# Decay factors made on the chip from three bfloat16 parts, weight slots placed by name, start and end reordered

## The chip, the cores and the metric

The kernel runs on one core of a Trainium2 chip. The metric is the device time of one execution in microseconds (us). Engines are called TensorE (PE in the rows, its weight loads PEld), VectorE (DVE), ScalarE (ACT), GpSimd (POOL) and SyncE (SP, which issues most of the DMAs). L12 is line 12 of the kernel before.

## What is computed

Three layers in a row, all in float32 at the border: retention (attention with a decay in place of the softmax), a mixture of eight experts with a skip, and a gated linear layer (GLU) with weights in float64. Cut to what matters:

```python
# retention: q, k, v are (4, 8, 576, 64)
scores = q @ k.transpose(0, 1, 3, 2) / sqrt(64)
gamma = 1 - 2.0 ** (-5.0 - arange(8))
ret = scores * where(i >= j, gamma ** (i - j), 0)
x = (ret @ v), as 2304 rows of 512
# experts: w1 (8, 512, 1024), w2 (8, 1024, 512)
for rows with x @ w_skip > 0:
    e = argmax(x @ w_gate); g = softmax(x @ w_gate)[e]
    x = x + g * (relu(x @ w1[e]) @ w2[e])
# GLU: w_a, w_b (512, 1536), w_out (1536, 512)
out = ((x @ w_a) * (x @ w_b)) @ w_out
```

## The kernel before

**Retention.** 18 tiles of 128 rows, nine to a pair of batches. The decay gamma^(i-j) is split: k is scaled by gamma^(-s) ahead of the transposes (`scale_k`, line 629, on GpSimd), and the output of a tile is multiplied by gamma^s / 8 (`decay`, line 721, VectorE). These second factors, `qt_sb`, are a table of 128 partitions by 4 head pairs by 576 positions in float32, 1.18 MB. It is loaded in four pieces (lines 758, 770, 773, 776). Tile i runs `scores` (line 673, then the mask product of line 676), q's transposes of a later pair of tiles (line 639, evicted in lines 647 on VectorE and 649 on ScalarE), k's transposes of tile i+1 (line 661, ScalarE eviction), `emit_x` of tile i-1 (line 741), `values` (lines 711 and 716) and `state` (line 691). A load of q serves two tiles.

**Start.** Lines 752 to 790 are written out by hand. All loads go through SP's queue, in this order: the key scales of consts_a, k of tile 0, consts (with the identity), q of tiles 0 and 1, the masks of consts_a, v, a table piece, k of tile 1, the routing weights, and so on. VectorE sets tiles to zero, ScalarE copies the identity into `xl_rhs`. TensorE multiplies an idle tile (`keep_warm`, line 134) eight times, transposes k, multiplies once more, transposes q in two halves, multiplies twice more, and then enters the loop.

**Experts.** Each expert runs the order of a plan, a string of names that `run_expert` goes through: F0 to F7 are the first products (line 503), S0 to S7 and Q0 to Q7 the second products for the first 128 rows and the 64 others (lines 517 and 535), E0 and E1 their evictions, X0 and X1 the transposes of the next expert's rows, N a gather, f, t and s the fetch, transposes and split of the GLU's first rows. `l` loads a quarter of a weight matrix of a later expert (line 202, 512 KB), `L` loads a piece of a GLU weight into a staging place (line 222, 512 KB), `gs` starts turning a staged piece into two fp32r parts and `gp` goes one step on with it. 36 such pieces make nine units of four. `split_wide` (lines 235 to 257) takes a piece of float64 apart with six VectorE instructions and three of ScalarE.

**Weight places.** Eight places of 8 KB a partition (`slots_a`) are taken in turn: expert e uses four, expert e+2 the same four again, so `l` in expert e loads for expert e+2. GLU units 0 to 4 have places of their own, units 5 to 8 take the turns after the last expert's, two each: units 5 and 6 the places of expert 6, units 7 and 8 those of expert 7. Up to 26 pieces may start before the GLU (`early`, line 1122).

**GLU.** Six groups of three tiles, twelve steps each. `glu_in` makes both products of a step (line 1239), ScalarE copies one (line 1243), VectorE multiplies (line 1244), and `split2` makes two fp32r parts (line 464 on ScalarE, line 465 on VectorE, in the first four steps on GpSimd). Then up to two remaining pieces are started and finished on the spot (`piece_pair(2)`, line 1291), and after that come the output products of the step before (`glu_out`, line 1256). The last step evicts three tiles (lines 1261 and 1263) and stores them from SP's queue; the last of them, tile 17, needs two transfers.

## Time and profile before

| | us |
|---|---|
| median of 3 runs | 766.37 |
| lowest, highest | 765.18, 767.53 |
| the profiled execution | 766.19 |
| its span, first to last instruction | 764.4 |
| TensorE busy in it | 745.5 |
| VectorE, ScalarE, GpSimd busy | 305.6, 230.1, 103.4 |
| DMA | 93.81 MB |

The busy time of TensorE is modelled at the ends of matmuls, so a full TensorE is not TensorE at its peak. In a row of a timeline the first number is the start in us from the span's start, the second the length of the merged group, and a bracket gives the idle time ahead of it and what ended that time. The granted clock is a share of 2.4 GHz.

### The profile page before, as it was taken

What the parts mean: (1) busy time and instruction counts of PE and PEld (TensorE: products, weight loads), DVE (VectorE), ACT (ScalarE), POOL (GpSimd) and SP (SyncE); (2) the same over time, 40 slices, a digit from 0 to 9 for tenths busy, and PEclk for the clock granted to TensorE, in tenths of its full rate; (3) what the DMA queues carried; (4) which work ended last, traced back from release to release, by engine and by line L of the source; (5) the groups of instructions that cost most, each with busy time, mean ns of one, the idle gap of its engine ahead of it and who ended that gap; (6) DMA issues with size and microseconds to landing.
All of it is one profiled execution on the core that took longest, in us unless ns stands there. A gap on an engine that the chain in (4) does not pass through costs nothing.

```text
span 764.4 us, 11767 instructions
## 1 busy us (share of the span) xinstructions
PE 745.5 (98%) x4753; PEld 652.8 (85%) x4753; DVE 305.6 (40%) x658; ACT 230.1 (30%) x482; POOL 103.4 (14%) x132
## 2 busy tenths in 40 slices
PE   8999998999999999999999999999999999999997
PEld 5889886766677777979999999999999999999996
DVE  5557664665666174982222222222222222222111
ACT  3445431444444153651221222121212121212111
POOL 1221111232211110140040004000400030001000
PEclk9999999999999999999999999999999999999999
DMA  9979997599998722440040004000400020001001
GB/s 229 228 189 251 276 318 260 182 380 360 343 347 302 223 78 75 136 140 1 1 124 0 1 1 125 1 0 1 124 4 25 14 83 1 1 1 42 1 1 41
DMA packets 89370, 93.81 MB, mean 123 GB/s; under 512 B 44833, under 2 KB 66977, under 8 KB 89314
## 3 DMA queue, kind: packets, MB, share of 16 engines
q1 hardware_dynamic: 84210, 78.07, 32.2%
q0 software_dynamic: 5104, 14.98, 6.3%
q8 instruction: 38, 0.62, 0.3%
q14 instruction: 18, 0.15, 0.1%
HBM read 80.02 MB, written 13.01 MB: 122 GB/s over the span
## 4 chain that ended last, share of the span: by engine, by line
PE 76%; DVE 3%; DMA 2%; issue 0%; ACT 0%; SPq 0%; ACTq 0%; DVEq 0%
PE ab L1239 36%; PE o L1256 18%; PE h L503 10%; PE y L517 6%; PE yr L535 4%; DMA st<-in_moe_w_out_dram 1%; PE pt L1104 1%; DVE mh L248 1%; PE xt L479 1%; DVE w L251 1%; DVE mh L243 1%; PE h L559 0%; DVE hb L241 0%; DMA y_dram<-yo 0%; DVE hb L252 0%
## 5 line engine op out<-in xcount | busy, mean ns | idle before, releaser
L1239 PE MATMUL ab<-xt,w 128*128 128x384 f32 x1728 | 313.0, 335 | 0.0
L1239 PEld LDWEIGHTS ab<-xt,w 128*128 128x128 f32 x1728 | 303.2, 188 | 6.5 <-issue 0.4
L1256 PE MATMUL o<-w,gg 128*128 128x512 f32 x648 | 163.5, 396 | 1.9 <-ACT gg L464 1.4
L1244 DVE TENSOR_TENSOR a_sb<-ab,a_sb 128x384 f32<-128x384 f32 x72 | 40.1, 557 | 276.0 <-PE ab L1239 250.9
L1256 PEld LDWEIGHTS o<-w,gg 128*128 128x128 f32 x648 | 119.2, 188 | 25.7 <-ACT gg L464 2.1
L1243 ACT ACTIVATE a_sb<-ab 128x384 f32<-128x384 f32 x72 | 35.3, 490 | 178.3 <-PE ab L1239 171.1
L464 ACT ACTIVATE gg<-a_sb 128x384 fp32r<-128x384 f32 x72 | 37.9, 526 | 163.6 <-DVE a_sb L1244 163.6
L503 PE MATMUL h<-xe,w 128*128 128x192 f32 x448 | 75.1, 328 | 0.0
L503 PEld LDWEIGHTS h<-xe,w 128*128 128x128 f32 x448 | 72.5, 190 | 3.0 <-issue 2.7
L517 PE MATMUL y<-w,ht 128*128 128x512 f32 x128 | 59.4, 598 | 0.0
L444 POOL DMA_INDIRECT out_dram<-ob,turns x15 | 14.8, 989 | 313.7 <-ACT ob L1263 311.5
L465 DVE TENSOR_TENSOR gg<-a_sb,gg 128x384 fp32r<-128x384 f32 x68 | 38.0, 559 | 40.3 <-ACT gg L464 37.9
L517 PEld LDWEIGHTS y<-w,ht 128*128 128x128 f32 x128 | 22.8, 190 | 20.3 <-issue 19.9
L251 DVE TENSOR_TENSOR w<-hb,st 128x512 fp32r<-128x512 f32 x36 | 24.8, 690 | 33.7 <-ACT st L246 33.4
L245 ACT ACTIVATE hb<-hb,ebias 128x512 int32<-128x512 int32 x36 | 25.8, 717 | 30.5 <-DVE hb L241 27.2
L438 POOL DMA_INDIRECT xg<-x_dram,list_i x15 | 15.0, 998 | 106.8 <-PE xt L479 56.7
L629 POOL TENSOR_TENSOR ks<-k,cst_a 128x512 f32<-128x512 f32 x18 | 18.8, 1043 | 78.0 <-DMA k<-in_k_dram 42.5
L506 ACT ACTIVATE ht<-h 128x384 f32<-128x384 f32 (+1 forms) x32 | 15.2, 475 | 45.1 <-PE h L503 45.1
L676 DVE TENSOR_TENSOR At<-s,cst_a 128x512 f32<-128x512 f32 x36 | 23.1, 684 | 10.6 <-PE s L673 10.6
L257 DVE TENSOR_TENSOR w<-mh,hb 128x512 fp32r<-128x512 f32 x36 | 24.3, 688 | 5.6 <-ACT mh L250 4.5
L535 PEld LDWEIGHTS yr<-w,ht 128*64 128x64 f32 x224 | 15.5, 137 | 12.4 <-DVE mh L248 3.8
L535 PE MATMUL yr<-w,ht 128*64 128x256 f32 x224 | 25.7, 382 | 0.0
(153 smaller groups left out, 639.8 us busy)
## 6 DMA issues: line engine op xcount, KB each, us to landing
w<-in_moe_w_dram SPq DMA_DIRECT2D x64, 512.0 KB
st<-in_moe_w_a_dram SPq DMA_DIRECT2D x12, 512.0 KB
st<-in_moe_w_b_dram SPq DMA_DIRECT2D x12, 512.0 KB
st<-in_moe_w_out_dram SPq DMA_DIRECT2D x12, 512.0 KB
x_dram<-xs SPq DMA_DIRECT2D x18, 256.0 KB
k<-in_k_dram SPq DMA_DIRECT2D x16, 256.0 KB
q<-in_q_dram SPq DMA_DIRECT2D x8, 512.0 KB
v<-in_v_dram SPq DMA_DIRECT2D x16, 256.0 KB
```

The costliest lines, as they stand in the source:

```text
L245: nc.scalar.activation(out=hb, in_=hb, func=ACTF.Relu, scale=8.0, bias=ebias)
L251: nc.vector.tensor_tensor(out=hi, in0=hb.bitcast(F32), in1=wh.bitcast(F32), op=ALU.mult)
L257: nc.vector.tensor_tensor(out=lo, in0=ml, in1=hb.bitcast(F32), op=ALU.mult)
L464: nc.scalar.activation(out=dst_hi, in_=src, func=ACTF.Copy)
L465: lo_engine.tensor_tensor(out=dst_lo, in0=src, in1=dst_hi, op=ALU.subtract)
L503: nc.tensor.matmul(ph[b][:, i], lhsT=w[:, c0:c0 + P], rhs=xh[:, kd], start=(kd == 0), stop=(kd == KD - 1), skip_group_check=True)
L517: nc.tensor.matmul(py[0], lhsT=ht[f][:, :P], rhs=w[:, f % 4], start=(f == 0), stop=(f == 7))
L535: nc.tensor.matmul(py[0][j * REST:(j + 1) * REST], lhsT=ht[f][:, at:at + REST], rhs=w[:, f % 4, j * half:(j + 1) * half], start=(f == 0), ...
L1239: nc.tensor.matmul(p, lhsT=w[a][:, kd, fc:fc + P], rhs=xt2[g][b][kd // 2][:, kd % 2], start=(j == 0), stop=(j == 3 * KD - 1))
L1243: nc.scalar.activation(out=a_sb, in_=pab[0], func=ACTF.Copy)
L1244: nc.vector.tensor_tensor(out=a_sb, in0=pab[1], in1=a_sb, op=ALU.mult)
L1256: nc.tensor.matmul(po[g][t], lhsT=gg[:, a, t * P:(t + 1) * P], rhs=w[b][:, f % 4], start=(f == 0 and j == 0), stop=(f == NF - 1 and j == 2))
```

## The change

**Decay factors.** The table is no longer loaded. Each factor is written on the host as three bfloat16 parts that sum to it exactly; a 24-row table of parts (8 heads by 3) with a 24-row selector of ones is loaded, 60 KB. Before the attention TensorE multiplies selector and table, 512 and 64 columns for each of four head pairs, and VectorE and ScalarE copy the sums from PSUM into `qt_sb`.

**Start.** k of tile 0 and q come first on SP's queue, q in two halves. The key scales, the part table, the identity and the masks come on ScalarE's queue; the rest of consts goes to SP behind the loads of tile 3. The memsets, the identity copies and `ut_bf` move to GpSimd, the first key scaling to VectorE. The idle products become 5, 2, 2 and 2. For tile 0 each half of q's transposes is evicted by both engines.

**Places by name.** Each weight unit has a fixed place. Expert 7 takes expert 6's four places, not expert 5's, so that GLU units 5 and 6 take those of expert 5, units 7 and 8 those of expert 7. Expert 5's plan loses its `l`. Up to 30 pieces may start before the GLU, and the plans of the last experts start and load them at other points. A strip of 120 floats (`rim`), which nothing used, goes.

**Pieces.** The scaling on ScalarE goes into VectorE's product. In the GLU one piece a step is started instead of two, and all subtractions of line 465 run on VectorE.

**End.** The last step takes its tiles in the order 2, 0, 1; the last one is evicted in halves by VectorE and ScalarE and stored from two queues.

```diff
+T_SEL = 0
+T_TAB = NP * P
+T_N = 5 * 256
...
-    slots_a = ctx.enter_context(tc.tile_pool(name="slots_a", bufs=NA))
+    slots_a = ctx.enter_context(tc.tile_pool(name="slots_a", bufs=1))
...
+    holder = [None] * NA
+    place = {n: (n % NA if n < 4 * (E - 1) else (n - 4) % NA) for n in range(4 * E)}
+    places_g = {}
+    for j, n in enumerate((4 * (E - 3), 4 * (E - 3) + 2, 4 * (E - 1), 4 * (E - 1) + 2)):
+        places_g[NB + j] = place[n], place[n + 1]
...
-    def turn_free(turn):
-        return turn == turns_taken[0] and (turn < NA or turn - NA in used)
...
+    def slot_free(n):
+        return holder[n] is None or holder[n] in used
+
+    def take_slot(n, dtype, who):
+        holder[n] = who
+        return slots_a.tile([P, 4, 512], dtype, tag=f"w{n}", name="w")
...
-        nc.scalar.activation(out=ml, in_=ml, func=ACTF.Copy, scale=2.0 ** -20)
...
-        nc.vector.tensor_tensor(out=lo, in0=ml, in1=hb.bitcast(F32), op=ALU.mult)
+        nc.vector.scalar_tensor_tensor(out=lo, in0=ml, scalar=2.0 ** -20, in1=hb.bitcast(F32),
+                                       op0=ALU.mult, op1=ALU.mult)
...
+    q_parts = at1.tile([3 * H, T_N // 2], F32, name="q_parts").bitcast(BF16)
...
-                nc.sync.dma_start(out=t, in_=q[2 * pr + c // 4, :, (c % 4) * P:(c % 4 + 2) * P, :].rearrange(
-                    "h (p r) d -> p h r d", r=2))
+                n = 4 if i == 0 else H
+                for h in range(0, H, n):
+                    nc.sync.dma_start(out=t[:, h:h + n], in_=q[2 * pr + c // 4, h:h + n,
+                                      (c % 4) * P:(c % 4 + 2) * P, :].rearrange("h (p r) d -> p h r d", r=2))
...
-        nc.gpsimd.tensor_tensor(out=t, in0=qkv["k", i], in1=kt.to_broadcast([P, H, D]), op=ALU.mult)
+        engine = nc.gpsimd if i else nc.vector
+        engine.tensor_tensor(out=t, in0=qkv["k", i], in1=kt.to_broadcast([P, H, D]), op=ALU.mult)
...
-                if g == 0:
+                if (r if i == 0 else g) == 0:
                     nc.vector.tensor_copy(dst, src)
...
-    nc.sync.dma_start(out=cst_a[:, :A_MASK], in_=consts_a[:, :A_MASK])
     load(0, 1)
-    nc.sync.dma_start(out=cst, in_=consts)
+    nc.scalar.dma_start(out=cst_a[:, :A_MASK], in_=consts_a[:, :A_MASK])
+    nc.scalar.dma_start(out=q_parts.bitcast(F32), in_=qtab)
+    nc.scalar.dma_start(out=ident, in_=consts[:, C_ID:C_ID + P])
     load(0, 0)
-    nc.sync.dma_start(out=cst_a[:, A_MASK:], in_=consts_a[:, A_MASK:])
+    nc.scalar.dma_start(out=cst_a[:, A_MASK:], in_=consts_a[:, A_MASK:])
     load(0, 2)
-    nc.sync.dma_start(out=qt_sb[:, :, :P], in_=qtab[:, :, :P])
     load(1, 1)
     for r in range(4):
-        nc.vector.memset(mbd[r], 0.0)
...
+        nc.gpsimd.memset(mbd[r], 0.0)
...
-    nc.sync.dma_start(out=qt_sb[:, :, P:2 * P], in_=qtab[:, :, P:2 * P])
     load(2, 0)
     load(2, 2)
-    nc.sync.dma_start(out=qt_sb[:, :, 2 * P:3 * P], in_=qtab[:, :, 2 * P:3 * P])
     load(3, 1)
     load(3, 2)
-    nc.sync.dma_start(out=qt_sb[:, :, 3 * P:], in_=qtab[:, :, 3 * P:])
+    nc.sync.dma_start(out=cst[:, :C_ID], in_=consts[:, :C_ID])
+    nc.sync.dma_start(out=cst[:, C_ID + P:], in_=consts[:, C_ID + P:])
...
     for a in range(KD):
-        nc.scalar.activation(out=xl_rhs[:, a, :P], in_=ident, func=ACTF.Copy)
-    nc.vector.tensor_copy(ut_bf, cst_a[:, A_UT:A_UT + P])
-
+        nc.gpsimd.tensor_copy(xl_rhs[:, a, :P], ident)
     scale_k(0)
+    nc.gpsimd.tensor_copy(ut_bf, cst_a[:, A_UT:A_UT + P])
     scale_k(1)
     warm = ps_x.tile([P, DM], F32, tag="x0", name="warm")
-    keep_warm(warm, 8)
+    keep_warm(warm, 5)
+
+    wide_banks = [(ps_s, "s0"), (ps_s, "s1"), (ps_k, "o"), (ps_o, "m")]
+    rest = ps_x.tile([P, NP, S - 512], F32, tag="x1", name="pq_rest")
+    for hp, (pool, tag) in enumerate(wide_banks):
+        pf = pool.tile([P, 512], F32, tag=tag, name="pf")
+        sel = q_parts[:, T_SEL + hp * P:T_SEL + (hp + 1) * P]
+        nc.tensor.matmul(pf, lhsT=sel, rhs=q_parts[:, T_TAB:T_TAB + 512], start=True, stop=True)
+        nc.tensor.matmul(rest[:, hp], lhsT=sel, rhs=q_parts[:, T_TAB + 512:T_TAB + S], start=True, stop=True,
+                         skip_group_check=True)
+        if hp % 2:
+            nc.scalar.activation(out=qt_sb[:, hp, :512], in_=pf, func=ACTF.Copy)
+        else:
+            nc.vector.tensor_copy(qt_sb[:, hp, :512], pf)
+    nc.vector.tensor_copy(qt_sb[:, :, 512:], rest)
+    keep_warm(warm, 2)
     k_transposes(0)
-    keep_warm(warm, 1)
+    keep_warm(warm, 2)
...
-    early = min(26, len(g_pieces))
+    early = min(30, len(g_pieces))
...
     NEXT_PLAN = (
-        "F0 F1 tk F2 F3 F4 tk F5 F6 F7 l l l l gs S0 S1 gp S2 "
-        "X0 S3 gp S4 X1 N gp S5 S6 gs S7 tk E0 gp Q0 Q1 gp Q2 Q3 l l gp Q4 gs Q5 Q6 gp Q7 l l E1 f2 f1 f0 "
+        "gs F0 gp F1 tk gp F2 gp L F3 gs F4 tk gp F5 gp F6 gp F7 l l l l gs L S0 S1 gp S2 "
+        "X0 S3 gp S4 X1 N gp S5 S6 S7 tk gs E0 gp Q0 Q1 Q2 gp Q3 l l Q4 gp L Q5 Q6 Q7 l l L E1 f2 f1 f0 "
     )
     LAST_PLAN = (
-        "gp F0 gs gp F1 gp F2 gp L F3 gs F4 gp F5 gp F6 t1 gp L F7 gs s1 S0 S1 gp t2 S2 "
-        "S3 gp s2 S4 S5 t0 gp L S6 s0 S7 E0 Q0 Q1 Q2 Q3 Q4 Q5 Q6 Q7 E1 "
+        "gs F0 gp F1 gp L F2 gs gp F3 gp F4 gp L F5 gs gp F6 gp t1 F7 gp L s1 S0 gs gp S1 t2 gp S2 gp L s2 "
+        "S3 gs S4 gp t0 S5 gp S6 s0 gp L S7 E0 Q0 Q1 Q2 Q3 Q4 Q5 Q6 Q7 E1 "
     )
...
-    plans = {0: FIRST_PLAN, 1: SECOND_PLAN, E - 2: NEXT_PLAN, E - 1: LAST_PLAN}
+    plans = {0: FIRST_PLAN, 1: SECOND_PLAN, E - 3: PLAN.replace("l ", ""), E - 2: NEXT_PLAN, E - 1: LAST_PLAN}
...
-        split2(gg[:, 0], gg[:, 1], a_sb, nc.gpsimd if g == 0 and f < 4 else nc.vector)
+        split2(gg[:, 0], gg[:, 1], a_sb)
...
-        for t in range(GT):
+        end = (g, f) == (NG - 1, NF - 1)
+        for t in (2, 0, 1) if end else range(GT):
...
+                if end and t == 1:
+
+                    (b, s0, p0, m), = seq_blocks(n)
+                    h = DM // 2
+                    nc.vector.tensor_copy(ob[:, :h], po[g][t][:, :h])
+                    nc.scalar.activation(out=ob[:, h:], in_=po[g][t][:, h:], func=ACTF.Copy)
+                    nc.sync.dma_start(out=out[b * S + s0:b * S + s0 + m, :h], in_=ob[:, :h])
+                    nc.scalar.dma_start(out=out[b * S + s0:b * S + s0 + m, h:], in_=ob[:, h:])
+                    continue
+                if t == (0 if end else 1):
                     nc.vector.tensor_copy(ob, po[g][t])
...
-                piece_pair(2)
+                piece_pair(1)
```

## Rows read from the trace of the kernel before

**Rows 1.** The page: busy us by engine, and the chain that ended last, by line.

```profile
PE 745.5 (98%) x4753; PEld 652.8 (85%) x4753; DVE 305.6 (40%) x658; ACT 230.1 (30%) x482; POOL 103.4 (14%) x132
...
PE ab L1239 36%; PE o L1256 18%; PE h L503 10%; PE y L517 6%; PE yr L535 4%; DMA st<-in_moe_w_out_dram 1%; PE pt L1104 1%; DVE mh L248 1%; PE xt L479 1%; DVE w L251 1%; DVE mh L243 1%; PE h L559 0%; DVE hb L241 0%; DMA y_dram<-yo 0%; DVE hb L252 0%
```

**Rows 2.** By stretch: length, busy PE, PEld, DVE, ACT, POOL, clock, DMA, GB/s.

```profile
0.00:20.00 20.00, 16.21 (x117) 10.99 (x118) 9.95 (x23) 7.40 (x18) 4.28 (x8) 1.00 0.91 226
150.00:200.00 50.00, 50.00 (x271) 37.31 (x270) 30.43 (x58) 23.32 (x43) 11.18 (x16) 1.00 1.02 370
276.30:298.70 22.40, 22.40 (x125) 16.70 (x125) 15.01 (x32) 11.24 (x23) 0.00 (x0) 1.00 0.29 89
303.40:310.60 7.20, 7.20 (x41) 6.81 (x40) 7.08 (x13) 4.40 (x9) 1.24 (x1) 1.00 0.19 62
```

**Rows 3.** Timeline of 0 to 30 us: start, length, engine, line, [idle before <-releaser].

```profile
1.21 3.60 PE L134 MATMUL warm<-idle_bf 128*128 128x512 bf16 x8 [1.21 <-DVE idle_bf L136]
...
4.50 1.04 POOL L629 TENSOR_TENSOR ks<-k,cst_a 128x512 f32<-128x512 f32 x1 [4.04 <-DMA k<-in_k_dram]
...
5.60 1.12 PE L661 MATMUL pk<-cst,ks 128*128 128x128 f32 x4 [0.79 <-POOL ks L629]
...
7.06 1.97 PE L639 MATMUL pq<-cst,q 128*128 128x128 f32 x8
...
8.21 1.75 DVE L647 COPY qT<-pq 64x256 f32<-64x256 f32 x4 [0.45 <-PE pq L639]
...
9.06 1.63 ACT L649 ACTIVATE qT<-pq 64x256 f32<-64x256 f32 x4 [1.72 <-PE pq L639]
...
11.28 1.29 DVE L676 TENSOR_TENSOR At<-s,cst_a 128x512 f32<-128x512 f32 x2 [1.32 <-PE s L673]
...
16.35 0.65 PE L639 MATMUL pq<-cst,q 128*128 128x128 f32 x4 [1.08 <-DMA q<-in_q_dram]
...
17.05 1.73 DVE L647 COPY qT<-pq 64x256 f32<-64x256 f32 x4 [0.46 <-PE pq L639]
...
18.57 0.39 SPq L607 DMA_DIRECT2D q<-in_q_dram  x1
...
24.26 0.63 PE L639 MATMUL pq<-cst,q 128*128 128x128 f32 x4 [1.24 <-DMA q<-in_q_dram]
```

**Rows 4.** Timeline of TensorE in the first GLU steps: output products, line 1256.

```profile
307.10 2.24 PE L1256 MATMUL o<-w,gg 128*128 128x512 f32 x9
...
313.37 2.24 PE L1256 MATMUL o<-w,gg 128*128 128x512 f32 x9
...
347.97 2.24 PE L1256 MATMUL o<-w,gg 128*128 128x512 f32 x9
```

**Rows 5.** Chain of waits followed back within 290 to 345 us: loads in it.

```profile
322.36 4.10 DMA st<-in_moe_w_out_dram
...
329.63 5.41 DMA st<-in_moe_w_out_dram
```

**Rows 6.** Timeline of all engines, 304 to 306 us.

```profile
304.26 0.42 DVE L243 TENSOR_SCALAR mh<-st 128x512 int32<-128x512 int32 x1
...
304.65 1.24 POOL L465 TENSOR_TENSOR gg<-a_sb,gg 128x384 fp32r<-128x384 f32 x1 [33.52 <-ACT gg L464]
304.93 1.25 DVE L243 TENSOR_SCALAR mh<-st 128x512 int32<-128x512 int32 x1
```

**Rows 7.** Timeline of all engines from 755 us to the end.

```profile
759.19 2.49 SPq L1269 DMA_DIRECT2D out_dram<-ob  x4
...
759.92 0.60 ACT L1263 ACTIVATE ob<-o 128x512 f32<-128x512 f32 x1 [0.76 <-PE o L1256]
```

**Rows 8.** Groups by line and form: busy us, mean ns of one, idle before.

```profile
L465 DVE TENSOR_TENSOR gg<-a_sb,gg 128x384 fp32r<-128x384 f32 x68 | 38.0, 559 | 40.3 <-ACT gg L464 37.9 <-issue 2.4
...
L248 DVE SCALAR_TENSOR_TENSOR mh<-st,mh 128x512 f32<-128x512 uint16 x36 | 24.5, 691 | 0.8
```

**Rows 9.** Chain of waits over the span: expert 6's first products.

```profile
254.19 10.60 PE h L503 x64
```

More of the change, by code (lines that the diff above doesn't have):

```diff
@@ L34 @@
 LINE = 512
-RIM = 120
 LATE = 15
@@ L97, in retention_moe_glu_kernel @@
     keep = ctx.enter_context(tc.tile_pool(name="keep", bufs=1))
-    rim = ctx.enter_context(tc.tile_pool(name="rim", bufs=1, side="right"))
-    rim.tile([P, RIM], F32, name="rim")
     edge = ExitStack()
     arena_p = ctx.enter_context(tc.tile_pool(name="arena_p", bufs=4, side="right"))
-    slots_a = ctx.enter_context(tc.tile_pool(name="slots_a", bufs=NA))
+    slots_a = ctx.enter_context(tc.tile_pool(name="slots_a", bufs=1))
     cv_p = edge.enter_context(tc.tile_pool(name="cv", bufs=2, side="right"))
@@ L181, in unit @@
         return units[u]
-    def turn_free(turn):
-        return turn == turns_taken[0] and (turn < NA or turn - NA in used)
-    def take_turn(dtype):
-        turns_taken[0] += 1
-        return slots_a.tile([P, 4, 512], dtype, tag="w", name="w")
+    def slot_free(n):
[3 more added lines that the diff above has]
+        return slots_a.tile([P, 4, 512], dtype, tag=f"w{n}", name="w")
     def load_m():
@@ L196, in load_m @@
         if u not in units:
-            assert turn_free(n), n
-            units[u] = take_turn(F32)
+            assert slot_free(place[n]), n
+            units[u] = take_slot(place[n], F32, n)
         dst = units[u].rearrange("p k f -> p (k f)")[:, cols]
@@ L270, in piece_start @@
             else:
-                turn = 4 * E + 2 * (n - NB)
-                if not (turn_free(turn) and turn + 1 - NA in used):
+                if not all(slot_free(j) for j in places_g[n]):
                     return False
-                units[u] = [take_turn(F32R) for _ in range(2)]
+                units[u] = [take_slot(j, F32R, u) for j in places_g[n]]
         st = staged.pop(i)
@@ L750, in emit_x @@
             nc.vector.tensor_reduce(out=lg[:, i], in_=xs[:, :, P:].rearrange("p a e -> p e a"), axis=AXX, op=ALU.add)
[L752 removed]
     load(0, 1)
[L754 removed]
+    nc.scalar.dma_start(out=cst_a[:, :A_MASK], in_=consts_a[:, :A_MASK])
+    nc.scalar.dma_start(out=q_parts.bitcast(F32), in_=qtab)
+    nc.scalar.dma_start(out=ident, in_=consts[:, C_ID:C_ID + P])
     load(0, 0)
[L756 removed]
+    nc.scalar.dma_start(out=cst_a[:, A_MASK:], in_=consts_a[:, A_MASK:])
     load(0, 2)
[L758 removed]
     load(1, 1)
     for r in range(4):
[L761 to L764 removed]
+        nc.gpsimd.memset(mbd[r], 0.0)
+    nc.gpsimd.memset(zero_row, 0.0)
+    nc.gpsimd.memset(ones_bf, 1.0)
+    nc.gpsimd.memset(ebias, -896.0 * 2.0 ** 23)
     nc.sync.dma_start(out=xl_rhs[:, :, P:P + 1],
@@ L1259, in glu_out @@
                 ob = ob_p[0].tile([P, DM], F32, tag="ob", name="ob")
-                if t == 1:
+                n = g * GT + t
+                if end and t == 1:
[7 more added lines that the diff above has]
+                if t == (0 if end else 1):
                     nc.vector.tensor_copy(ob, po[g][t])
@@ L1334, in shape_constants @@
     s = np.arange(S)
-    qt = gam[:, None] ** s[None, :] / np.sqrt(D)
-    qt = qt.reshape(NP, 2, 1, S).repeat(D, axis=2).reshape(NP, P, S).transpose(1, 0, 2)
-    return c.astype(f), ca.astype(f), np.ascontiguousarray(qt).astype(f)
+    part = (gam[:, None] ** s[None, :] / np.sqrt(D)).astype(f)
+    tab = np.zeros((3 * H, T_N), np.uint16)
+    for j in range(3):
+        top = (part.view(np.uint32) >> 16).astype(np.uint16)
+        tab[j::3, T_TAB:T_TAB + S] = top
+        part = part - (top.astype(np.uint32) << 16).view(f)
+    assert not part.any()
+    one = np.float32(1.0).view(np.uint32) >> 16
+    for h in range(H):
+        p0 = T_SEL + h // 2 * P + h % 2 * D
+        tab[3 * h:3 * h + 3, p0:p0 + D] = one
+    return c.astype(f), ca.astype(f), tab.view(f)
 _INS = [
```

5 lines of the change are left out of this document (removed).

## Prediction

> **What bounds the kernel now.** I read the page's busy line and its chain first [rows 1]. TensorE is busy 745.5 of 764.4 us, and the chain that ended last lies mostly on it, 36% in the gate and value products of the GLU (line 1239), 18% in its output products (line 1256). So an edit pays only where TensorE is short of work, or where it takes matmuls away, and this one takes none away. Next I read the table of stretches [rows 2]: in 150 to 200 us TensorE is busy all the time; in the first 20 us it is busy 16.21, with the DMA engines at 0.91. Then the timelines at the places where TensorE waits and the change reaches: the first 25 us [rows 3], the first GLU steps [rows 4 to 6], and the last 6 us [rows 7]. There the reader should look at the brackets, which say what TensorE waited for.
>
> **Start: what is there.** The first state that everything hangs on is the first mask product of VectorE at 11.28 us [rows 3]. Before it, q's transposes run at 7.06, their evictions go wholly to VectorE (8.21, 1.75 us) for the first half and wholly to ScalarE (9.06, 1.63 us) for the second, so ScalarE is done at 10.69, and the scores end about 0.6 later. Afterwards TensorE waits twice for a load of q: 1.08 us at 16.35 and 1.24 us at 24.26, while SP issued the second of these at 18.57 only [rows 3]. After 24.26 it waits for no load in the attention.
>
> **Start: the loads.** The table's 1.18 MB leave SP's queue and a table of 61 KB comes on ScalarE's, as do both pieces of consts_a and the identity. At the 226 GB/s of the first 20 us [rows 2] the 1.1 MB are 5 us of transfer, most of it ahead of the load at 18.57. So that load can land some 4 to 6 us earlier, more than its 1.24 us wait: gain 1.24. At 16.35 half a megabyte of table is gone from ahead, some 2.3 us, more than the 1.08 waited; but the next transposes wait for VectorE's copies (17.05, 1.73 us) and these stand behind the mask product of their own step, which ends 0.46 us before them. So only about 0.5 of the 1.08 comes back. Together 1.7 us, between 1.2 and 2.3.
>
> **Start: the products.** Before the transposes stand, new on TensorE, four products of 512 columns and four of 64. What level TensorE runs at must be read from spacing: four transposes of one shape take 1.12 us at 5.60 and 0.65 at 16.35 [rows 3], though the granted clock is given as 1.00 in this stretch [rows 2]. So the first 9 us run at half speed, 1.2 GHz. The eight idle products of 512 columns at 1.21 took 3.60 us [rows 3], 0.43 each; with 0.05 for 64 columns the new ones are 1.92 us in all; two idle products more before k's transposes and one more behind them than before. The parts table is the second DMA on ScalarE's queue; k, the second on SP's, was used at 4.50 [rows 3], so I let the products begin at 4.4 (bounds 3.5 and 4.9). Then in TensorE's order: products 1.92, two idle products 0.85, k's transposes 0.85, two idle products 0.85, q's first four transposes from 8.87 to 9.72, the others to 10.57. q has landed by then (its first half moves from fourth to second place on SP's queue, and it was used at 7.06). Each half is now evicted by both engines, two copies of 0.43 each (a quarter of 1.75): the first 10.0 to 10.9, the second 10.9 to 11.75, mask product at 12.3: 1.0 us later than now. If the speed doubles from q's transposes on, 11.9: 0.6 later. With the early bound and an early doubling, 11.0: 0.3 earlier; with the late one, 1.5 later. I take 0.7 later, nearest to the rows at half speed. The five evictions of the table (0.6 to 0.7 us each by the mask products and the 0.60 in [rows 7], two engines) lie under these idle products and transposes. So the start gives 1.7 - 0.7 = 1.0 us, between -0.3 and 2.6. The Trainium skill (TensorE: Matmul & The Clock Gate, part 1) says that the throttled level is the default and that activity releases it; the trace agrees in the spacing at 5.60 and 16.35. By that rule the added products, which close a gap in TensorE's work, would bring the release forward, which is the 0.6 or the 0.3 rather than the 1.0.
>
> **Start: GpSimd and VectorE.** The first key scaling moves to VectorE and so leaves GpSimd's 1.04 us [rows 3] for about 0.65, half of the two mask products' 1.29; it is done near 5, long before k's transposes at 7.2. The memsets, identity copies and ut cast go to GpSimd. No row shows their price there; at no more than the scaling's 1.04 us for 512 elements four memsets are 4.2 us and four quarter-size copies 1.0, done by about 8, and the second key scaling behind them is wanted after the first scores, past 11: cost 0. If that cover goes, at most 1 us. ScalarE issues four DMAs ahead of its first work, the evictions near 6, and has nothing else to do until then. The masks are the last of the four and wanted at 11.28; the rest of consts goes behind the loads of the fourth tile on SP and is first read by the routing, tens of us later: 0. What speaks against this move is a row of the GLU: VectorE's line 243 took 1.25 us beside a GpSimd subtraction of 1.24, against 0.42 just before [rows 6]. The Trainium skill (SBUF — State Buffer, Who interferes with whom) has the rule for it: the two engines share a port pair, and whoever comes second is held. By it the first key scaling would be held by at most one identity copy, which ends before TensorE wants it; the sum stays.
>
> **Experts.** In `split_wide` a ScalarE scaling, one in each of 36 pieces, goes into VectorE's product that follows, whose new form takes 0.691 us in line 248 [rows 8]. Both lie beside TensorE, ScalarE being busy 30% of the span [rows 1]: cost and gain 0. Slots by name let pieces 20 to 27 be turned in experts 5 and 6 already, 30 pieces before the GLU where 26 stood. What a piece costs VectorE I take from the first GLU step: 7.08 us busy in 7.2 [rows 2] are one product of 0.56 (as the subtraction of that shape, 0.559 [rows 8]), two pieces and the 0.83 by which one instruction was held [rows 6], so 2.85 a piece. The last expert gets five pieces where VectorE works at about four now; its 15.01 us busy in 22.4 [rows 2] become 17.9. It then still ends with the expert, and x's split for the GLU is late by nothing, by 0.7 us if it waits for a load on the way. The price of the slots: expert 7's weights take expert 6's places. Its first matrix can be issued only when expert 6's first products end, 254.19 + 10.60 = 264.79 [rows 9], and is wanted where expert 7's stretch begins, at 276.3 [rows 2], 11.5 us later. Four loads make 2.1 MB, three gathers of x rows beside them 0.8; at the 370 GB/s of 150 to 200 us [rows 2] 7.8 us. A lone 512 KB load took 4.10 and 5.41 us [rows 5], of which 1.4 would be its bytes at that rate, so 2.7 to 4 us come on top: 10.5 to 11.8. Late by 0 to 0.3; I take 0. What waits behind these loads on SP is the write of y and two piece loads, which nobody wants for 4 us and more. The second matrix is issued by 276.3 and wanted after expert 7's first products, 10.6 us later: 0.
>
> **GLU.** A step is 6.27 us (313.37 - 307.10) [rows 4]. From 307.10 to 347.97 lie six steps, 40.87 where 37.62 would do: 3.25 lost. The reason is ten pieces left for the first five steps, two in each: VectorE is busy 7.08 us with one product and two pieces [rows 2], more than a step, and it waits for loads of w_out that SP could issue only when a staging place came free, 4.10 and 5.41 us [rows 5]. After the change six pieces are left, one a step: product 0.56, subtraction 0.56, piece 2.85, 4.0 in all, with the ScalarE waits inside a piece under 5.5. Each load then has two or three steps to land. The GpSimd subtraction of 1.24 us becomes that one of 0.56, and line 243 is freed of its 0.83. What is late next is TensorE itself. Gain 3.25, between 2.0 and 3.25.
>
> **End.** The order 2, 0, 1 sends the block with two transfers out first. The last eviction began at 759.92 and took 0.60; halves take 0.30 to 0.45. SP issued four transfers in 2.49 us from 759.19 [rows 7], the last at about 761.1; now its last starts near 760.6 beside ScalarE's. Gain 0.5, between 0 and 1.0; no row shows a transfer on ScalarE's queue.
>
> **Sum.** 1.0 + 0 + 3.25 + 0.5 = 4.75 us. The profiled execution took 766.19 us (span 764.4 and 1.8 around it), the median of the runs is 766.37, 0.2 above. 766.19 - 4.75 = 761.4.
>
> **Rivals.** (1) The start gives nothing or costs: the products and idle matmuls run at the low level and the queue of TensorE, not q, sets the first scores, 1.5 us late, and only 0.5 to 1.2 of the waits comes back. Then 763.0. For it speaks the 1.12 us at 5.60, against it that q's waits are gone for certain. (2) The conversion still gates the GLU: VectorE comes 1 to 2 us late out of expert 7 and the steps go on at its pace; of the 3.25 one is left: 764 to 764.5, within no change. Against it speak the 4.0 us of work in a 6.27 us step. (3) Slower: expert 7's weights are late. At a rate r the 2.9 MB arrive 2.9/r + 2.7 us after 264.79; what passes 11.5 us stops TensorE in whole. At 212 GB/s the 4.75 us are eaten, at 181 the kernel is 2.3 slower, 768.7. For it speaks the 226 GB/s of the first 20 us, against it that those are packets of 256 and 512 bytes, and 370 GB/s with weights. (4) Better: the first scores 0.3 early and both waits gone whole, 2.6, the end 1.0: 759.3.
>
> **How the numbers follow.** About 0.3%, 2.3 us, is what a measurement of this kernel can tell from no change. Forecast 761.4 with 0.60; (1) 0.14; (2) 0.11; (3) 0.06, (4) 0.09. All bounds at once give 759.3 to 764.8. The range 759.0 to 764.5 takes in the forecast, (1) and (4) and half of (2), and leaves out the rest of (2) and (3). Faster by over 0.3% (below 764.1): the forecast, (1), (4), some of (2): 0.85. Same 0.10, slower 0.05.
>
> **What would show it.** Right: no q wait at the second and fourth tile; the mask product between 11.0 and 12.5; output products 6.27 us apart from the first GLU step on; TensorE without a gap at expert 7's start and at its second products; the last SP issue 0.5 us closer to the last matmul. Wrong: a TensorE wait for w in expert 7, VectorE still the releaser in the first GLU steps, or q's transposes beginning after 10.

## The result, and the profile after

The changed kernel takes 760.13 us (median of 4 runs, 759.69 to 760.88) beside 766.95 for the kernel before: a ratio of 0.9916, 95% interval 0.9895 to 0.9936. The forecast was 761.4 us, range 759.0 to 764.5, faster. The profiled execution took 759.69 us with a span of 757.8, so the span lost 6.6 us where the sum has 4.75. The sign is right and the size near, but not term by term. The changed kernel is called after in what follows, the kernel before is called before.

The page of after: busy us by engine, and the chain that ended last.

```profile
PE 741.6 (98%) x4761; PEld 652.5 (86%) x4761; DVE 307.1 (41%) x659; ACT 211.9 (28%) x444; POOL 100.6 (13%) x139
...
PE ab L1262 40%; PE o L1280 19%; PE h L508 10%; PE y L522 7%; PE yr L540 4%; PE pt L1127 1%; PE xt L484 1%; PE h L564 0%; PE xt L1127 0%; PE xt L573 0%; DVE ob L1289 0%; ACT ob L1290 0%
```

TensorE is busy 3.9 us less than in [rows 1], though no matmul was taken away; that is the first sign of something which the sum doesn't have. The timeline of the first 30 us of after (start, length, engine, line, [idle before <- releaser]):

```profile
4.22 0.60 PE L800 MATMUL pf<-q_parts 24*128 24x512 bf16 x1 [0.70 <-DMA q_parts<-qtab_dram]
...
7.08 1.06 PE L670 MATMUL pk<-cst,ks 128*128 128x128 f32 x4
...
8.78 1.54 PE L648 MATMUL pq<-cst,q 128*128 128x128 f32 x8
...
9.88 1.73 DVE L656 COPY qT<-pq 64x256 f32<-64x256 f32 x4 [3.04 <-PE pq L648]
...
10.83 1.69 ACT L658 ACTIVATE qT<-pq 64x256 f32<-64x256 f32 x4 [2.06 <-DVE qT L656]
...
11.28 2.00 PE L682 MATMUL s<-qT,kT 64*128 64x128 f32 x16 [0.52 <-ACT qT L658]
...
13.11 1.29 DVE L685 TENSOR_TENSOR At<-s,cst_a 128x512 f32<-128x512 f32 x2 [1.50 <-PE s L682]
...
16.43 0.40 SPq L615 DMA_DIRECT2D q<-in_q_dram  x1
...
17.02 0.66 PE L648 MATMUL pq<-cst,q 128*128 128x128 f32 x4
...
20.20 0.63 PE L648 MATMUL pq<-cst,q 128*128 128x128 f32 x4 [1.14 <-DVE qT L656]
...
24.23 0.66 PE L648 MATMUL pq<-cst,q 128*128 128x128 f32 x4
```

This answers [rows 3]. The first factor product starts at 4.22 and q's transposes at 8.78, where 4.4 and 8.87 were worked out, and neither 17.02 nor 24.23 has a wait for q any more. But ScalarE's evictions begin at 10.83, behind VectorE's first two, and the first mask product comes at 13.11, 1.83 us later than in [rows 3]. TensorE in the first GLU steps of after:

```profile
298.46 8.59 PE L1262 MATMUL ab<-xt,w 128*128 128x384 f32 x48
306.89 2.20 PE L1280 MATMUL o<-w,gg 128*128 128x512 f32 x9
...
313.10 2.20 PE L1280 MATMUL o<-w,gg 128*128 128x512 f32 x9
...
344.13 2.20 PE L1280 MATMUL o<-w,gg 128*128 128x512 f32 x9
```

The first GLU product comes at 298.46; in before it came at 298.66. So all of the attention and the experts gave 0.2 us between these two traces. From there on, output products stand 6.21 us apart (344.13 - 306.89 is six steps of 6.21) without a gap; in [rows 4] a good step is 6.27, and of the six from 307.10 to 347.97 four are longer. The stretches of the last expert and of the first GLU step (columns as in [rows 2]):

```profile
276.30:298.70 22.40, 22.40 (x125) 16.80 (x125) 18.16 (x39) 10.34 (x21) 0.00 (x0) 1.00 0.71 249
303.40:310.60 7.20, 7.20 (x41) 6.85 (x40) 5.37 (x11) 2.94 (x6) 5.13 (x6) 1.00 0.54 173
```

VectorE has 18.16 us in the first (forecast 17.9) and 5.37 of 7.2 in the second, where it had 7.08. The end of after, in answer to [rows 7]:

```profile
752.72 0.42 DVE L1289 COPY ob<-o 128x256 f32<-128x256 f32 x1
753.18 0.38 ACT L1290 ACTIVATE ob<-o 128x256 f32<-128x256 f32 x1 [1.22 <-DVE ob L1289]
753.60 0.36 ACTq L1292 DMA_DIRECT2D out_dram<-ob  x1
753.79 0.45 SPq L1291 DMA_DIRECT2D out_dram<-ob  x1
```

VectorE's half is done at 753.14, and ScalarE's, of the same length nearly, begins only then. From the first eviction of the last tile to the end of the span it is 757.8 - 752.72 = 5.1 us; in before it was 764.4 - 759.92 = 4.5.

The GLU makes the rest. From its first product to its last output product's start it is 460.8 us in before and 453.8 in after, 7.0 less: 3.3 for the stalls and 3.7 for steps that are shorter throughout. The groups of line, engine and form show the second (busy us, mean ns of one | idle before), first before, then after. `ab<-xt,w` are the gate and value products, whose moving operand is a tile of x's halves (xt); `o<-w,gg` are the output products, which read only weights and gg, the two parts of the gated product:

```profile
L1239 PE MATMUL ab<-xt,w 128*128 128x384 f32 x1728 | 313.0, 335 | 0.0
...
L1256 PE MATMUL o<-w,gg 128*128 128x512 f32 x648 | 163.5, 396 | 1.9 <-ACT gg L464 1.4 <-POOL gg L465 0.4
```

```profile
L1262 PE MATMUL ab<-xt,w 128*128 128x384 f32 x1728 | 311.6, 336 | 0.0
...
L1280 PE MATMUL o<-w,gg 128*128 128x512 f32 x648 | 160.2, 392 | 0.0
```

The same 1728 and 648 matmuls are 1.4 and 3.3 us shorter, the 3.3 with about 1 us of stalls in it. So the account of the span is: start 0.2, GLU stalls 3.3, shorter steps 3.7, end -0.6, together 6.6.

### The profile page after: what moved, and what is told of

The parts are those of the page before. It is cut to its first block, busy times and chain, and to the rows that moved or that the text cites. A ratio compares the mean times of both kernels' runs of the same rounds, so it can differ in the third digit from the quotient of the medians.

```text
span 757.8 us, 11716 instructions
## 1 busy us (share of the span) xinstructions
PE 741.6 (98%) x4761; PEld 652.5 (86%) x4761; DVE 307.1 (41%) x659; ACT 211.9 (28%) x444; POOL 100.6 (13%) x139
## 4 chain that ended last, share of the span: by engine, by line
PE 82%; DVE 0%; ACT 0%; issue 0%
PE ab L1262 40%; PE o L1280 19%; PE h L508 10%; PE y L522 7%; PE yr L540 4%; PE pt L1127 1%; PE xt L484 1%; PE h L564 0%; PE xt L1127 0%; PE xt L573 0%; DVE ob L1289 0%; ACT ob L1290 0%
## 5 line engine op out<-in xcount | busy, mean ns | idle before, releaser
L1262 PE MATMUL ab<-xt,w 128*128 128x384 f32 x1728 | 311.6, 336 | 0.0
L1280 PE MATMUL o<-w,gg 128*128 128x512 f32 x648 | 160.2, 392 | 0.0
L470 DVE TENSOR_TENSOR gg<-a_sb,gg 128x384 fp32r<-128x384 f32 x72 | 40.2, 558 | 42.5 <-ACT gg L469 39.6
L254 DVE SCALAR_TENSOR_TENSOR mh<-st,mh 128x512 f32<-128x512 uint16 x36 | 25.0, 696 | 1.2
```

The source lines that it names most:

```text
L254: nc.vector.scalar_tensor_tensor(out=ml, in0=h1, scalar=2.0 ** -16, in1=mh, op0=ALU.mult, op1=ALU.add)
L470: lo_engine.tensor_tensor(out=dst_lo, in0=src, in1=dst_hi, op=ALU.subtract)
L1262: nc.tensor.matmul(p, lhsT=w[a][:, kd, fc:fc + P], rhs=xt2[g][b][kd // 2][:, kd % 2], start=(j == 0), stop=(j == 3 * KD - 1))
L1280: nc.tensor.matmul(po[g][t], lhsT=gg[:, a, t * P:(t + 1) * P], rhs=w[b][:, f % 4], start=(f == 0 and j == 0), stop=(f == NF - 1 and j == 2))
```

## Experiments

A name with b_ is the kernel before with an edit, a name with a_ the changed kernel with one.

**What makes the GLU step shorter.** Four things in it differ: the strip, the places of the last weight units, the pieces, the subtraction's engine. The strip of 120 floats stood ahead of all pools of the right side, so without it x's halves for the GLU lie 480 bytes further; weights, gg and PSUM tiles of the first steps lie where they lay. The staging and conversion tiles and the output buffers of that side move as well, but of what moved only x's halves are read in every step. First the kernel before without it (b_nostrip):

```diff
-    rim = ctx.enter_context(tc.tile_pool(name="rim", bufs=1, side="right"))
-    rim.tile([P, RIM], F32, name="rim")
```

> The kernel before without the strip of 120 floats, nothing else changed. The GLU step went from 6.27 us before to 6.21 after, 72 times, which is 3.8 us that the forecast does not have. Theory A: the strip sets where x's halves for the GLU lie (480 bytes further when it is gone), and the products that read them run quicker at the new place. Then output products follow each other 6.21 us apart here too, once the pieces are done, the stalls of the first five steps stay, and the time is 766.9 - 3.8 = 763.1. Theory B: the gain comes from the weight places or from the pieces, and the strip is nothing. Then the steps stay at 6.27 and the time at 766.9 within 0.5.

Measured: 763.32 us beside 766.47, ratio 0.9955 (0.9937 to 0.9972). And the other way round, the two lines put into the changed kernel (a_strip):

> The changed kernel with the strip of 120 floats put back, nothing else changed. Theory A (the place of x's halves sets the length of a GLU step): steps of 6.27 us instead of 6.21, the first GLU product where it was at 298.5, time 760.1 + 3.8 = 763.9. Theory B (weight places or pieces do it): steps of 6.21 and 760.1 within 0.5.

Measured: 763.63 us beside 766.47, ratio 0.9964 (0.9947 to 0.9981). The groups of a_strip:

```profile
L1264 PE MATMUL ab<-xt,w 128*128 128x384 f32 x1728 | 313.0, 336 | 0.0
...
L1282 PE MATMUL o<-w,gg 128*128 128x512 f32 x648 | 162.5, 395 | 0.0
```

With the strip after has before's gate and value products, 313.0, and its output products are 2.3 us longer; together 3.7 us, and the two medians agree with theory A to 0.3 us. The groups of b_nostrip:

```profile
L1237 PE MATMUL ab<-xt,w 128*128 128x384 f32 x1728 | 311.7, 336 | 0.0
...
L1254 PE MATMUL o<-w,gg 128*128 128x512 f32 x648 | 162.0, 395 | 2.2 <-POOL gg L463 2.2
```

311.7 where after has 311.6, and 162.0 with a stall of 2.2 that is still there. The execution in this trace is the slowest of its twelve (767.21), and the granted clock was 0.50 from 327 to 329 us, right behind that stall, which lengthens the 162.0; from 333.70 on, output products stand 6.2 us apart. The strip alone makes the step, in both directions; the weight places and the pieces have no part in it. In detail, the output products of a plain step start on average 229, 233, 236, 224, 231, 236, 228 and 233 ns apart with the strip (a_strip), and 227 or 228 throughout without it (after). But after has the slow spacing too: in the 15 steps where the four transposes of line 1127 stand right ahead of the output products, these start 230, 235, 231, 230, 231, 230 and 227 ns apart behind a first gap of 314, with the same tiles at the same places. So the place of their own operands doesn't settle the spacing of the output products; what runs just before them bears on it too.

**Which places are slow.** Shorter strips in the changed kernel, 8 floats (a_strip8) and then 16 (a_strip16) in place of 120:

> The changed kernel with a strip of 8 floats, 32 bytes, so that x's halves begin 448 bytes past the place that they had before instead of 480. With 480 the spacing of the output products is 227 ns, with 0 it is 231 in a pattern of 224 to 236. Theory A (a multiple of 64 bytes is the slow place, 448 is one, 480 is not): 231 ns, steps of 6.27, 763.6. Theory B (only a larger power of two is slow): 227 ns, steps of 6.21, 760.1.

> The changed kernel with a strip of 16 floats, 64 bytes: x's halves begin 416 bytes past their old place, 32 past a multiple of 64 as in after, where they began at 480. With 0 and with 448, both multiples of 64, the GLU step is longer: at 0 the output products stand 231 ns apart, at 448 these keep 227 and the gate and value products go from 173.6 to 176.7. Theory A (multiples of 64 bytes are the slow places): spacings of 227 and 173.6 and 760.1. Theory B (480 is a place of its own, the other places differ each in its own way): at least one of the two spacings longer than in after, 761 or more.

One execution each: 764.55 and 761.75 us. The groups of a_strip8, then of a_strip16:

```profile
L1264 PE MATMUL ab<-xt,w 128*128 128x384 f32 x1728 | 316.5, 338 | 0.0
...
L1282 PE MATMUL o<-w,gg 128*128 128x512 f32 x648 | 160.4, 392 | 0.0
```

```profile
L1264 PE MATMUL ab<-xt,w 128*128 128x384 f32 x1728 | 311.6, 336 | 0.0
...
L1282 PE MATMUL o<-w,gg 128*128 128x512 f32 x648 | 162.5, 395 | 0.0
```

Gate, value and output products together take 475.5 us at 0 bytes (a_strip), 474.1 at 416, 476.9 at 448 and 471.8 at 480 (after). At 448 it is the gate and value products that are long (316.5), at 416 the output products (162.5), which don't read the tile that was moved at all, and at 0 both (313.0 and 162.5). So the rule of 64 bytes fell: 416 should have been quick. Four places and four lengths are what the runs show, two of them in one execution each; what decides is open.

**What the GLU stalls hung on.** One number in the kernel before, and the same number back in the changed one. First the kernel before (b_pair1):

```diff
-                piece_pair(2)
+                piece_pair(1)
```

> The kernel before with one piece started in each of the first GLU steps instead of two, nothing else. Ten pieces are then spread over nine steps: VectorE has one product and one piece in each, 4 us against a step of 6.27. Theory A (the pairing is what costs the 3.25 us of the first five steps): the stalls are gone without any of the earlier conversions, 766.5 - 3.25 = 763.2. Rival B (the loads of w_out that wait for a staging place cost it, and thus the ten pieces themselves): one or two stalls of 1 to 2 us stay, 764.5 to 765.5.

Measured: 762.83 us beside 766.79, ratio 0.9934 (0.9912 to 0.9957). Its output products:

```profile
306.93 2.24 PE L1256 MATMUL o<-w,gg 128*128 128x512 f32 x9
...
313.20 2.24 PE L1256 MATMUL o<-w,gg 128*128 128x512 f32 x9
...
344.53 2.24 PE L1256 MATMUL o<-w,gg 128*128 128x512 f32 x9
```

They stand 6.27 us apart from the first on (344.53 - 306.93 is six steps), with ten pieces left, GpSimd's subtraction and all the old plans. From first GLU product to last output product it is 457.55 us, 3.29 less than before: the whole term. Now two a step in the changed kernel (a_pair2):

> The changed kernel with two pieces started in each of the first GLU steps again, nothing else. Six pieces then fall on three steps, in which VectorE has 0.56 + 0.56 + 2 x 2.85 = 6.8 us of work against a step of 6.21. Theory A (the pairing costs): stalls of 0.6 us and more in the first three steps, 1 to 2 us in all, 761 to 762. Rival B (the number of pieces left costs, not their pairing): the six are loaded ahead, VectorE has slack from the steps before, and the time stays at 760.1.

Measured: 765.10 us beside 766.79, ratio 0.9968 (0.9945 to 0.9992): 5 us above after, more than either theory has. The chain of waits of a_pair2, followed back within 303 to 330 us, has this load in it:

```profile
309.56 7.12 DMA st<-in_moe_w_out_dram
```

And its timeline, VectorE's first piece instruction in the third step and TensorE's output products behind it, then a stretch right behind that (columns as in [rows 2]):

```profile
316.70 0.43 DVE L247 TENSOR_SCALAR hb<-st 128x512 int32<-128x512 int32 x1 [2.15 <-DMA st<-in_moe_w_out_dram]
...
323.07 3.94 PE L1280 MATMUL o<-w,gg 128*128 128x512 f32 x9 [2.65 <-ACT gg L469]
```

```profile
324.00:327.00 3.00, 3.00 (x8) 2.32 (x8) 2.97 (x7) 2.84 (x5) 0.00 (x0) 0.50 0.02 5
```

The load of w_out was issued when a staging place came free at 309.56 and was used 7.12 us later. A second piece a step wants it within one step of 6.21; VectorE waits 2.15 us, has two pieces to do ahead of the step's own product, and TensorE waits 2.65. Then the granted clock falls: 1.00 from 317 to 323 us, 0.50 from 324 to 327, 1.00 again from 328 on, and the nine output products take 3.94 us for 2.20. The next group of nine comes at 331.14, 8.07 us later where a step has 6.21. So the third step's wait costs 2.8 us and the lower clock behind it 1.9, together 4.7 of the 5; neither theory had the late load or the clock. At one piece a step the same load has two steps. So it is the pairing that costs, not the number left, and of TensorE's wait VectorE's own wait for a load, 2.15 us, is the larger part, not its busy time.

**Both together.** The kernel before with these two edits and nothing else (b_both):

> The kernel before with only two edits: no strip, and one piece a step in the GLU instead of two. Alone, each gave 3.2 us (763.32 beside 766.47) and 4.0 us (762.83 beside 766.79). Theory A: these two are the whole gain of the change, and start, weight places, plans and end add nothing: 766.6 - 7.2 = 759.5, output products 6.21 us apart from the first step on. Rival: the two gains share something, or the rest of the change adds a microsecond that the start and the end take back: 761 to 762.

Measured: 759.71 us beside 766.31, ratio 0.9909 (0.9872 to 0.9945). Its groups:

```profile
L1237 PE MATMUL ab<-xt,w 128*128 128x384 f32 x1728 | 311.6, 336 | 0.0
...
L1254 PE MATMUL o<-w,gg 128*128 128x512 f32 x648 | 160.2, 392 | 0.0
```

They are those of after to 0.1 us, and from the first GLU product to the last tile's eviction it is 454.3 us in both (754.46 - 300.14 here, 752.72 - 298.46 in after). Two edits of one or two lines give what the change gives; factors by products, slots by name, plans, order of loads and the new end add nothing that these times can show.

**The start.** The changed kernel with the whole old start (table loads, old order, old engines; a_oldstart):

> The changed kernel with the whole old start: the table of decay factors loaded in four pieces, the old order of loads and idle products, the memsets, copies and first key scaling on their old engines, tile 0 evicted by halves. By the forecast the new start is worth 1.0 us: 761.1, and the first GLU product 1.0 later than 298.5. By the two traces it is worth 0.1, since the mask product came 1.83 later and the two waits for q gave just that back: 760.2, first GLU product at 298.6, mask product near 11.3 and waits of about 1.1 us for q at the second and fourth tile.

Measured: 760.31 us beside 766.47, ratio 0.9909 (0.9881 to 0.9938), 0.2 from after. The new start is worth nothing that can be measured, and not the 1.0 of the forecast. The execution that was profiled took 763.0, with a granted clock of 0.91 in the first 20 us, so its trace only tells that the two waits for q are back (1.19 us at 17.60, 1.53 at 25.81) and nothing of the typical mask product. In seven traces with the new start unchanged the first GLU product comes between 297.96 and 299.42, so tenths of a microsecond between single traces say nothing of the start. Then only the sharing of the first tile's evictions undone (a_halves):

```diff
-                if (r if i == 0 else g) == 0:
+                if g == 0:
```

> The changed kernel, but the first tile's transposes of q evicted as before: the first half of four wholly by VectorE, the second wholly by ScalarE, which lie in different PSUM banks. In after both engines share each half, and ScalarE's copies began at 10.83 only, when VectorE's two of the same half were done. Theory A (two engines on one PSUM bank are put behind each other): here both engines run side by side, ScalarE ends near 12.0 instead of 12.52, the mask product comes at 12.5 instead of 13.11, and the time is 759.6, half a microsecond under after. Rival: the scores are held by TensorE's own queue at the low clock level, and the mask product stays at 13.1, time 760.1. Second rival: it comes earlier, but a later wait for VectorE's copies at 20 us eats it: mask product at 12.5, time 760.1.

Measured: 759.96 us beside 766.79, ratio 0.9890 (0.9851 to 0.9930). The timeline of a_halves:

```profile
9.05 1.92 PE L648 MATMUL pq<-cst,q 128*128 128x128 f32 x8
...
10.14 1.75 DVE L656 COPY qT<-pq 64x256 f32<-64x256 f32 x4 [3.04 <-PE pq L648]
...
11.00 1.64 ACT L658 ACTIVATE qT<-pq 64x256 f32<-64x256 f32 x4 [1.96 <-PE pq L648]
...
13.23 1.29 DVE L685 TENSOR_TENSOR At<-s,cst_a 128x512 f32<-128x512 f32 x2 [1.33 <-PE s L682]
```

Now the engines run side by side, but the eight transposes took 1.92 us instead of 1.54, ScalarE waited for TensorE until 11.00, and the mask product came at 13.23, where the seven traces with the new start have 12.84 to 13.33. Theory A of this run fell in this execution, and it is TensorE's queue ahead of the scores that its first rival names. Whether sharing a bank would cost at an equal clock, one look at each can't say. So the products were taken out of that queue (a_spread): made a tile at a time, the first group (four products of 128 columns, one eviction) behind q's transposes in place of the two idle products, the others within the first tile; eight idle products ahead as before, q's transposes evicted as in a_halves, and the old end.

```diff
-    keep_warm(warm, 5)
+    keep_warm(warm, 8)
...
+    factors(0, ps_o, "m", False)
...
+            factors(1, ps_x, "x0", False)
+            factors(2, ps_x, "x1", True)
...
+            factors(3, ps_t, "tq", False)
...
+            factors(4, ps_x, "x1", False)
```

> The changed kernel with the old end and with the products of the decay factors spread: eight idle products as before ahead of k's transposes, q's transposes evicted by halves on two engines, and the factors made a tile at a time (128 columns of the four head pairs in one bank, one eviction), the first behind q's transposes, three more within the first tile, the last behind its state. After had all eight products ahead of k's transposes, at the low clock level, and its mask product came at 13.11. Theory A: k's transposes come at 5 instead of 7.1, the mask product at 11.3 to 11.8, the five small groups take 0.3 each of TensorE in the first tile, and with the old end 758.5 to 759 comes out. Rival: TensorE, having done less before q's transposes, stays longer at the low level, the mask product comes at 12.5 or later, and the time is that of the old end alone, 759.6.

Measured: 758.60 us beside 766.31, ratio 0.9892 (0.9862 to 0.9923). Timeline of its start, then TensorE's first GLU product:

```profile
5.44 1.09 PE L670 MATMUL pk<-cst,ks 128*128 128x128 f32 x4 [0.63 <-DMA cst<-consts_dram]
...
7.17 1.92 PE L648 MATMUL pq<-cst,q 128*128 128x128 f32 x8
...
9.02 0.45 PE L799 MATMUL pf<-q_parts 24*128 24x128 bf16 x4
...
9.71 1.80 PE L682 MATMUL s<-qT,kT 64*128 64x128 f32 x16 [0.24 <-DVE qT L656]
...
11.34 1.29 DVE L685 TENSOR_TENSOR At<-s,cst_a 128x512 f32<-128x512 f32 x2 [1.32 <-PE s L682]
...
12.03 0.61 PE L799 MATMUL pf<-q_parts 24*128 24x128 bf16 x8
```

```profile
297.80 2.52 PE L1267 MATMUL ab<-xt,w 128*128 128x384 f32 x13
```

k's transposes come at 5.44, 1.64 us ahead of after's, the mask product at 11.34, 1.77 ahead, and the first GLU product at 297.80, 0.7 ahead. The small groups of products now lie on TensorE's path within the first tile: from their starts (12.03, 13.70 and 14.64) to the next matmul it is 0.54, 0.32 and 0.22 us, 1.1 in all, which is the difference. The earlier mask product is clear of the 12.84 to 13.33 of the seven traces; the 297.80 lies only just under their 297.96 to 299.42. It has the lowest median of all here, 1.5 under after's, 0.5 of which the old end alone gave too (a_oldend below), and the two intervals overlap: that the spread products are quicker over the whole kernel is not shown.

**The end.** The old end in the changed kernel, and the new order with one whole eviction and one transfer (a_oldend, then a_whole):

> The changed kernel with the old end: tiles 0, 1, 2 in order, one eviction each, all stores on SP. By the forecast the new end is worth 0.5 us, so this would take 760.6. By the trace of after, in which ScalarE's half of the last eviction began only when VectorE's was done and 5.1 us lie between the last matmul's end and the end of the span against 4.5 before, the new end costs 0.6, so this would take 759.5.

> The changed kernel with the last tile evicted whole by ScalarE and stored in one transfer, tiles still in the order 2, 0, 1. The old order with whole evictions took 759.59 in the run before, 0.5 less than after. Theory A: the order is worth what the forecast says (one transfer is issued behind the last eviction instead of two), and the halves are what costs, since the second waits for the first and its transfer is issued last: 759.1, and the last transfer issued 1.1 us behind the last matmul. Rival: the order is what costs (whatever ends the span is the landing of a transfer, and the order makes no difference to that): 760.1.

Measured: 759.59 us beside 766.47, ratio 0.9903 (0.9873 to 0.9932), and 759.70 beside 766.79, ratio 0.9889 (0.9852 to 0.9927). Timelines of the ends, a_oldend and then a_whole:

```profile
751.85 2.49 SPq L1292 DMA_DIRECT2D out_dram<-ob  x4
...
752.58 0.60 ACT L1286 ACTIVATE ob<-o 128x512 f32<-128x512 f32 x1 [0.76 <-PE o L1279]
```

```profile
751.50 2.25 SPq L1293 DMA_DIRECT2D out_dram<-ob  x4
...
752.24 0.60 ACT L1288 ACTIVATE ob<-o 128x512 f32<-128x512 f32 x1 [0.76 <-PE o L1280]
```

From the last tile's first eviction to the end of the span it is 757.1 - 752.58 = 4.5 us with the old end, 756.9 - 752.24 = 4.7 with the order alone, and 5.1 with the halves. The order gives nothing, the halves cost 0.4; theory A of the second run fell in its first part. In the medians half a microsecond can't be told, so the rows carry this, and they repeat: 4.5 in each of six traces with the old end, 5.1 in each of seven with the halves. The reason that theory A gives for the halves fell as well. In after it is not ScalarE's transfer that is issued last but SP's, at 753.79, 0.65 us behind the end of VectorE's half, since SP was still issuing the three transfers before it. Counted from the last tile's first eviction, the last issue ends at 1.76 us with the old end, 1.51 with the order alone and 1.52 with the halves; the last packet lands at 3.18, 3.33 and 3.35; and from there to the end of the span it is 1.32, 1.32 and 1.75. So the issue that the order brings ahead is lost in the landing, and the 0.4 of the halves lies behind the last packet. The version with halves is also the only one of the three that stores from ScalarE's queue; what takes the 0.4 is open.

## Why the prediction was right, point by point

**Bound and method.** An edit pays where TensorE is short of work: this held for the GLU stalls. It failed where it says that the edit takes nothing away from TensorE itself, since the same matmuls followed each other at another spacing (227 ns for 231 in the output products).

**Start, 1.0 forecast, 0.2 measured.** The loads were right: 1.7 us were to come back behind the first mask product, and from there to the first GLU product it is 287.38 us in before and 285.35 in after, 2.0 less, and the two waits for q are gone. At 20.20 a wait for VectorE's copies stays, as the text has it. The products were mis-sized: 0.7 later was taken, with 1.5 as the late bound, and it was 1.83. The start and length of each step on TensorE came within 0.2 us; the step that failed is the pair of evictions in which both engines work on one half at the same time (10.0 to 10.9 and 10.9 to 11.75). ScalarE ended at 12.52, and the mask product missed the window of 11.0 to 12.5 that the text gives as a sign. Undoing the sharing brought the mask product no earlier (a_halves, 13.23, with slower transposes), so what sharing alone costs is not shown. The Trainium skill (PSUM — Partial Sum Buffer, PSUM bank collisions raise a hardware error) says that two engines must not be on the same bank and quadrant of partitions at once, that reads count too, and that the tools put such instructions behind each other. The trace agrees at the end, where both halves lie in the same partitions: ScalarE's began at 753.18, 0.04 us behind VectorE's. At the start the engines read different halves of the partitions, which the page would let run together; here they did not, and ScalarE's first copy at 10.83 began 0.09 us behind VectorE's two of that half. Writing one tile of SBUF is not enough for that: in [rows 3] both engines write q's tile at once (8.21 to 9.96 and 9.06 to 10.69). But in after the two also write columns that alternate, so that the bank is the reason at the start is likely, not shown.

**Experts, 0.** Right. There is no wait of TensorE at expert 7's start or in it (22.40 us busy of 22.40), with 249 GB/s moved in its stretch; the rival with late weights (0.06) fell, and VectorE's 18.16 us were 17.9 in the text.

**GLU stalls, 3.25.** Right in size: 3.3. But the text credits more than is needed. It lets the four pieces fewer, the subtraction on VectorE and the one piece a step act together; one piece a step does it alone (b_pair1). Of its two reasons, VectorE's 7.08 us and the loads that wait for a staging place, a_pair2 shows the load as the larger, 2.15 of the 2.65 us that TensorE waited. The rival in which the conversion still gates the GLU (0.11) fell; its 764 to 764.5 doesn't follow from its own terms, since 766.19 - 1.0 - 1.0 - 0.5 is 763.7.

**The strip, 0.** This term is missing. The text says nothing of the strip, which nothing used, and takes 6.27 us for a step after the change as well as before. It is the largest single gain, 3.7 us; without it the time would have been 763.6 (a_strip), and the forecast 2 us too low.

**End, 0.5.** Wrong in sign, -0.6. The order was costed as moving the last issue ahead. It does, by 0.25 us (1.76 to 1.51 behind the last tile's first eviction), but the last packet lands no earlier. The halves were costed as running together, 0.30 to 0.45; one behind the other they took 0.84, but that didn't reach the end either, since SP issued the last transfer only when its other three were out. The 0.4 that the halves cost lies behind the last packet and has no term in the text.

So the GLU stalls were forecast for their reason, but that the whole sum came near is luck: a missing gain of 3.7 covers 0.8 that the start and 1.1 that the end fell short.

## What to carry to other kernels

When a step that recurs dozens of times changes its length, compare the spacing of its matmuls before looking for waits, and move the place of its operands by some tens of bytes as an experiment of its own. Two engines on one PSUM bank did not halve an eviction here, at either place; splitting by bank was tried once and showed no gain. Before conversions are moved across stages, try spreading what is left over the steps: here a load that had two steps to land cost nothing, and one that had a single step cost 2.8 us and 1.9 more at the lower clock behind it.

## What the runs showed of the hardware

**The spacing of matmuls depends on where an operand lies, and on what ran before.** Moving the moving operand of the gate and value products by 480 bytes changed the 2376 GLU matmuls from 475.5 to 471.8 us at a granted clock of 1.00, and most of it in the output products, which read other tiles (231 to 227 ns apart). Places of 416 and 448 bytes gave 474.1 and 476.9. With nothing moved, the output products of after stand mostly 230 to 235 ns apart instead of 227 where four transposes run right ahead of them. So the other group may feel the move through what precedes it; that, and why the spacing has these two levels, is open.

**A load of 512 KB took 7.12 us from issue to use** in the GLU, where [rows 5] show 4.10 and 5.41; SP issued a second load with it, and two gathers were issued beside it.

**A stall can cost more than its wait.** In a_pair2 TensorE waited 2.65 us, and the granted clock was 0.50 from 324 to 327 us, right behind; in b_nostrip it waited 2.24 us, and the clock was 0.50 from 327 to 329. Behind the wait of 1.40 us in before (341.47) it stayed at 1.00.

**The low clock level ends at different moments.** The same eight transposes took 1.54 us at 8.78 in after, 1.19 at 8.82 in a_oldend, which has the same start, and 1.92 at 9.05 in a_halves and at 7.17 in a_spread. A start that is worked out at one level for a whole row of instructions is off by some tenths.

**The end repeats to hundredths.** From the last tile's first eviction to the end of the span it was 4.48 to 4.51 us in six traces with the old end and 5.06 to 5.10 in seven with the halves, though the times of single executions differ by microseconds.
